# Routing of the first expert half spread over rounds 4 to 8 of the attention, with some of its steps on GpSimd and other places for the gathers

## The chip, the cores and the metric

The kernel runs on one core of one Trainium2 chip. TensorE (PE) multiplies, VectorE (DVE), ScalarE (ACT) and GpSimd (POOL) work element by element, SyncE (SP) only issues DMAs. The metric is the device time of one execution in microseconds (us), as the median of several runs.

## The reference

```python
def _attn_ref(q, k, v, w_phi):                 # q, k, v: 4 x 8 heads x 576 x 64, w_phi: 64 x 128
    def phi(x):
        proj = np.einsum('bhsd,df->bhsf', x, w_phi)
        proj = proj - np.max(np.abs(proj), axis=-1, keepdims=True)
        return np.concatenate([np.exp(proj), np.exp(-proj)], axis=-1)
    q_p, k_p = (phi(q), phi(k))
    kv = np.einsum('bhsf,bhsd->bhfd', k_p, v)
    z = np.sum(k_p, axis=2)
    num = np.einsum('bhsf,bhfd->bhsd', q_p, kv)
    den = np.einsum('bhsf,bhf->bhs', q_p, z)[..., None] + 1e-06
    return (num / den).astype(np.float32)
...
x = np.ascontiguousarray(attn_out.transpose(0, 2, 1, 3)).reshape(B * S, H * D)   # 2304 tokens x 512
logits = x @ w_gate + modality_bias[modality_id]                                 # 8 experts
e_idx = np.argmax(logits, axis=1)
gate_w = probs[np.arange(N), e_idx]
...
    h = np.maximum(x[mask] @ w1[e], 0.0)                                         # per expert, F = 1024
    out[mask] = gate_w[mask, None] * (h @ w2[e])
...
return ((x @ w_a) * (x @ w_b) @ w_out).astype(np.float32)                        # d_ff = 1536
```

## The kernel before

The kernel has three stages, one after the other on TensorE: the attention (to about 167 us), the experts (`Moe`, to about 390 us) and the gated layer (`Moe2`, to the end).

**Attention.** A unit `u` is one pair of batches and one pair of heads; there are eight. `Attn.round(r)` for r = 0 to 8 works on unit r and finishes unit r-1. In a round, `phi` projects a piece of q or k (tile pjp on TensorE; on VectorE the maximum m and the difference df), `turn` transposes parts of df (qtp, then the exponentials qts on ScalarE), `kx` makes the 64x73 products (kxp, copied by VectorE to kx), `vg` the gate products of v (vgp, copied into v), `num` multiplies qts by kx (nmp; VectorE divides: rec, x), and `store` writes x to DRAM (xs) and lets GpSimd add the gate logits (lgp). TensorE's order is that in which the code is written; VectorE, ScalarE, GpSimd and SP are put in an order by a scheduler when the kernel is built. Their order is fixed from then on: each engine runs its list and waits at an instruction until what it needs is there. PSUM tiles come from three pools of two buffers each: pjp, "q" (qtp) and "c" (kxp, vgp, nmp).

**Routing.** The logits of units 0 to 3 are those of the first 1152 tokens, which is half of them. `Route` turns them into tables: `gate` and `score` pick the expert, `rank` counts by matmuls (rkp), `place` and `where` give each token its place (pl, col), `bounds` the tiles' experts and ends (meta), `table` the token of each place (tbp, idx) and `back` the place of each token (tbq, perm, and the gate weights g2). `lookup` is a matmul of one-hot tables. For the first half these are made on GpSimd, by 9 instructions for each table (tbph, tbpl and their product tbpr for `table`; tbqh, tbql, tbqr for `back`). The steps are hung into the rounds by a table: `aside(0)` comes after kx(r-1, 1), `aside(1)` after num and store of unit r-1, `aside(2)` at the end of a round.

**Experts.** A tile is 608 tokens of one expert. `gather` reads its tokens from xs in five indirect DMAs of GpSimd (128 tokens each, the last 96; tile xg), `transp` turns them (mxt on TensorE, then mxh on ScalarE and mxl on VectorE; two PSUM buffers), `l1` and `l2` multiply by weights (hp, yp) that are loaded by SP (s) and split into two parts (wh, wl). The first tile's gathers and transposes lie in the attention's last two rounds. `issue_after(i)` keeps the scheduler from placing an instruction ahead of i; it is no wait on the chip.

Of the kernel before, what the change touches and what calls it, by code (L numbers as in the profile page):

```python
# [12 lines left out]
BF16 = mybir.dt.bfloat16  # L13
I32 = mybir.dt.int32
AF = mybir.ActivationFunctionType
ALU = mybir.AluOpType
# [4 lines left out]
P = 128  # L21
# [4 lines left out]
E = 8  # L26
# [32 lines left out]
class Attn:  # L59
# [159 lines left out]
    def num(self, u, *parts):  # L219
# [20 lines left out]
        for b, h in parts:  # L240
            k = 4 if b < 2 else 2
            nc.vector.tensor_mul(x[:, 4 * b:4 * b + 4, h, :] if b < 2 else x[:, 8, :, :], ps[:, o:o + k, 0:72],
                                 rec[:, o:o + k].unsqueeze(2).to_broadcast([P, k, 72]))
            o += k

    def store(self, u):
# [89 lines left out]
class Route:  # L336
    def __init__(self, tc, pool, lgp, bs, bp):
        self.tc, self.nc = tc, tc.nc
        self.pool, self.lgp, self.bs, self.bp = pool, lgp, bs, bp

    def steps(self, wk, ps, tag, after=None):
# [6 lines left out]
        return [start, self.gate, self.score, self.rank, self.place, self.where, self.bounds, self.table, self.back]  # L348
# [4 lines left out]
    def gate(self):  # L353
        nc, c = self.nc, self.cst
# [6 lines left out]
        nc.vector.tensor_copy(mf, mi)  # L361
        tmp = self.w([NG, E], "bstmp")
        sel = self.w([NG], "bsel")
        for m in range(2):
            nc.vector.tensor_scalar(out=sel, in0=mf, scalar1=float(m), scalar2=None, op0=ALU.is_equal)
            nc.vector.tensor_mul(tmp, sel.unsqueeze(2).to_broadcast([P, NG, E]),
                                 bb[:, m, :].unsqueeze(1).to_broadcast([P, NG, E]))
            nc.vector.tensor_add(lg, lg if m else self.lgp, tmp)
        self.lg = lg

    def score(self):
# [4 lines left out]
        ex = self.w([NG, E], "bstmp")  # L376
# [10 lines left out]
    def rank(self):  # L387
# [9 lines left out]
        gt = self.gt = self.w([NG], "gt")  # L397
        nc.vector.tensor_reduce(out=gt, in_=self.ex, op=ALU.add, axis=AX.X)
        nc.vector.tensor_scalar_add(gt, gt, 1e-9)
        nc.vector.reciprocal(gt, gt)  # L400

    def place(self):
# [8 lines left out]
        pf = self.w([2, E], "pf")  # L411
# [3 lines left out]
        self.tv, self.pf, self.vals = tv, pf, self.w([3, NG], "vals")  # L415
# [33 lines left out]
    def bounds(self):  # L449
        nc, c, tv, pf = self.nc, self.cst, self.tv, self.pf  # L450
# [5 lines left out]
        lo = self.w([NTMAX, E], "lo")  # L456
        hi = self.w([NTMAX, E], "hi")
        te_, of_ = pf[:, 0, :], pf[:, 1, :]
        end = self.w([E], "end")
        nc.vector.tensor_add(end, te_, tv[:, 0, :])  # L460
        it = c["it"].unsqueeze(2).to_broadcast([P, NTMAX, E])
        meta = self.w([3 * NTMAX + 1], "meta")
        nc.vector.tensor_tensor(out=lo, in0=it, in1=te_.unsqueeze(1).to_broadcast([P, NTMAX, E]), op=ALU.is_ge)
        nc.vector.tensor_tensor(out=hi, in0=it, in1=end.unsqueeze(1).to_broadcast([P, NTMAX, E]), op=ALU.is_ge)
        nc.vector.tensor_reduce(out=meta[:, :NTMAX], in_=hi, op=ALU.add, axis=AX.X)
        nc.vector.tensor_scalar(out=meta[:, :NTMAX], in0=meta[:, :NTMAX], scalar1=float(E - 1), scalar2=None, op0=ALU.min)
        nc.vector.tensor_sub(lo, lo, hi)
        b2 = self.w([E], "b2")
        nc.vector.scalar_tensor_tensor(out=b2, in0=te_, scalar=-float(TS), in1=of_, op0=ALU.mult, op1=ALU.add)
        nc.vector.tensor_add(hi, c["ittS"].unsqueeze(2).to_broadcast([P, NTMAX, E]),  # L470
                             b2.unsqueeze(1).to_broadcast([P, NTMAX, E]))
        nc.vector.tensor_mul(hi, hi, lo)
        nc.vector.tensor_reduce(out=meta[:, NTMAX:2 * NTMAX], in_=hi, op=ALU.add, axis=AX.X)
        nc.vector.tensor_scalar(out=meta[:, 2 * NTMAX:3 * NTMAX], in0=meta[:, NTMAX:2 * NTMAX], scalar1=float(CG),
                                scalar2=float(HALF), op0=ALU.add, op1=ALU.min)
        nc.vector.tensor_copy(meta[:, 3 * NTMAX:], end[:, E - 1:E])
# [33 lines left out]
    def table(self):  # L510
# [3 lines left out]
        hi, lo = self.lookup("tbp", self.col, n, self.pl, self.toks)  # L514
        self.token(self.idx, hi, lo, 0)

    def back(self, ps=None, tag=None):
        nc = self.nc
        gp = self.w([3, NG], "gp", BF16)
        rest = self.w([NG], "grest")  # L520
        nc.vector.tensor_copy(rest, self.gt)
        for i in range(3):
            nc.vector.tensor_copy(gp[:, i, :], rest)
            if i < 2:
                nc.vector.tensor_sub(rest, rest, gp[:, i, :])
# [613 lines left out]
```

## Time and profile before

| | us |
|---|---|
| three runs | 814.98, 816.0, 819.0 |
| median | 816.0 |
| the profiled execution | 819.03 |
| its span, first to last instruction | 817.2 |
| mean granted TensorE clock | 0.995 of full speed |

TensorE is busy for 799.0 us of the span, VectorE for 602.8, ScalarE for 376.6 and GpSimd for 136.3. Times in the rows further down are microseconds from the start of the span. In a row of the timeline the bracket tells how long the engine had been idle and which instruction ended that.

### The profile page before, as it was taken

The numbers are of one execution on the slowest core, as the hardware profiler recorded it, in microseconds if no ns is written. First come the engines' busy times: TensorE is split into PE (matmuls) and PEld (weight loads), VectorE is DVE, ScalarE is ACT, GpSimd is POOL, SyncE is SP. The second block draws the span as 40 slices with busy tenths as digits, with TensorE's granted clock in tenths as the row PEclk, the third lists the DMA queues.
The fourth block names the chain that finished last, engine by engine and source line by source line (L and its number), as shares of the span: only waits on it lengthen the run. The fifth ranks groups of instructions, "written<-read, shape, count | busy, mean of one in ns | idle before, by whom it ended". The sixth has DMA issues, their size and how long they took to land.

```text
span 817.2 us, 18324 instructions
## 1 busy us (share of the span) xinstructions
PE 799.0 (98%) x7283; PEld 752.5 (92%) x7284; DVE 602.8 (74%) x1071; ACT 376.6 (46%) x666; POOL 136.3 (17%) x164
## 2 busy tenths in 40 slices
PE   8999998899999999999999999999999999999996
PEld 7999888799999999999999999999999999999995
DVE  6888899599999999974588897764555585544553
ACT  4556544544445555543445444543333364333333
POOL 2000009532326532200112020030000002000002
PEclk9999999999999999999999999999999999999999
DMA  8765432476579887763789787876566658665642
GB/s 304 215 192 162 154 111 82 131 258 198 209 285 338 330 294 274 255 238 114 271 323 364 261 309 260 272 274 202 185 229 205 198 184 302 207 199 193 214 130 89
DMA packets 85163, 184.22 MB, mean 225 GB/s; under 512 B 27760, under 2 KB 37520, under 8 KB 85072
## 3 DMA queue, kind: packets, MB, share of 16 engines
q1 hardware_dynamic: 81872, 173.21, 62.2%
q0 software_dynamic: 3040, 9.72, 3.4%
q8 instruction: 58, 0.95, 0.5%
q14 instruction: 33, 0.27, 0.1%
q10 hardware_dynamic: 160, 0.07, 0.0%
HBM read 145.21 MB, written 37.75 MB: 224 GB/s over the span
## 4 chain that ended last, share of the span: by engine, by line
issue 46%; POOL 3%; PE 2%; POOLq 0%; ACT 0%; ACTq 0%
POOL out L853 2%; POOL cvs L717 1%; PE abp L54 1%; PE abp L56 1%; PE abp L55 1%; POOLq L1136 0%; PE op L55 0%; PE op L54 0%; PE op L56 0%; ACT cvs L716 0%; POOLq L853 0%; POOLq L717 0%; ACTq L884 0%; ACT pc L897 0%
## 5 line engine op out<-in xcount | busy, mean ns | idle before, releaser
L897 ACT COPY pc<-abp 128x384 f32<-128x384 f32 x252 | 120.9, 480 | 193.7 <-PE abp L56 189.7
L54 PE MATMUL abp<-yh,fw 128*128 128x384 f32 x504 | 170.1, 337 | 1.5 <-ACTq L1062 1.0
L56 PE MATMUL abp<-yh,fw 128*128 128x384 f32 x504 | 170.0, 337 | 0.0
L55 PE MATMUL abp<-yl,fw 128*128 128x384 f32 x504 | 169.8, 337 | 0.0
L54 PEld LDWEIGHTS abp<-yh,fw 128*128 128x128 f32 x504 | 94.6, 188 | 10.6 <-ACT pc L897 1.3
L55 PEld LDWEIGHTS abp<-yl,fw 128*128 128x128 f32 x504 | 94.7, 188 | 7.5
L717 POOL TENSOR_SCALAR cvs<-cvs 128x768 f32<-128x768 f32 x24 | 60.3, 2511 | 218.0 <-ACT cvs L716 217.9
L56 PEld LDWEIGHTS abp<-yh,fw 128*128 128x128 f32 x504 | 94.6, 188 | 0.0
L55 PE MATMUL op<-fw,gh 128*128 128x512 f32 x216 | 85.7, 397 | 0.0
L54 PE MATMUL op<-fw,gh 128*128 128x512 f32 x216 | 85.1, 394 | 0.0
L56 PE MATMUL op<-fw,gl 128*128 128x512 f32 x216 | 85.0, 394 | 0.0
L55 PE MATMUL yp<-hl,wh 128*128 128x304 f32 x256 | 77.4, 303 | 0.8 <-DVE hl L608 0.8
L54 PE MATMUL hp<-mxh,wh 128*128 128x304 f32 x256 | 78.0, 305 | 0.0
L55 PE MATMUL hp<-mxl,wh 128*128 128x304 f32 x256 | 77.8, 304 | 0.0
L56 PE MATMUL hp<-mxh,wl 128*128 128x304 f32 x256 | 77.7, 304 | 0.0
L56 PE MATMUL yp<-hh,wl 128*128 128x304 f32 x256 | 77.6, 304 | 0.0
L54 PE MATMUL yp<-hh,wh 128*128 128x304 f32 x256 | 77.0, 303 | 0.0
L853 POOL DMA_INDIRECT out<-o,perm x18 | 18.4, 1020 | 310.6 <-ACT o L852 303.1
L190 ACT ACTIVATE qts<-qtp 128x512 f32<-128x512 f32 (+1 forms) x80 | 38.3, 557 | 58.3 <-PE qtp L187 50.2
L908 DVE TENSOR_TENSOR d<-u,pc 128x768 f32<-128x768 f32 x36 | 34.4, 957 | 28.8 <-ACT pc L897 28.8
L885 DVE TENSOR_TENSOR gl<-ca,gh 128x384 fp32r<-128x384 f32 x72 | 40.8, 574 | 16.4 <-ACT gh L884 15.4
L156 DVE TENSOR_REDUCE m<-pjp 128x8 f32<-128x1024 f32 (+2 forms) x49 | 45.1, 934 | 9.5 <-PE pjp L154 9.5
(191 smaller groups left out, 1595.7 us busy)
## 6 DMA issues: line engine op xcount, KB each, us to landing
fw<-wsc SPq DMA_DIRECT2D x72, 512.0 KB
fw<-wsc SPq DMA_DIRECT2D x144, 256.0 KB
raw<-in_moe_w SPq DMA_DIRECT2D x24, 768.0 KB
s<-in_moe_w SPq DMA_DIRECT2D x32, 512.0 KB
fw<-wsc SPq DMA_DIRECT2D x72, 128.0 KB
wsc<-whi SPq DMA_DIRECT2D x12, 640.0 KB
wsc<-wsum SPq DMA_DIRECT2D x12, 640.0 KB
wsc<-whi SPq DMA_DIRECT2D x12, 512.0 KB
```

What stands on the lines that cost most here:

```text
L54: nc.tensor.matmul(out, lh, rh, start=start, stop=False)
L55: nc.tensor.matmul(out, lh, rl, start=False, stop=False)
L56: return nc.tensor.matmul(out, ll, rh, start=False, stop=stop).ins
L156: nc.vector.tensor_reduce(out=mv, in_=pv, op=ALU.max, axis=AX.X, apply_absolute_value=True)
L190: nc.scalar.activation(t[:, s, :n, :], ps[:, :n, :], AF.Exp, scale=1.0 - 2.0 * s)
L717: nc.gpsimd.tensor_scalar(out=s.bitcast(F32), in0=s.bitcast(F32), scalar1=LEAST, scalar2=None, op0=ALU.max)
L853: st = nc.gpsimd.indirect_dma_start(out=self.out[:, :], out_offset=bass.IndirectOffsetOnAxis(ap=self.routes[bp].perm[:, c:c + 1], axis=0), ...
L885: self.gl = nc.vector.tensor_sub(gl, ca[:, i, :], f32(gh)).ins
L897: self.copied = copied = nc.scalar.copy(x, ps).ins
L908: nc.vector.tensor_add(d, u, x.unsqueeze(1).to_broadcast([P, 2, n]))
```

## The change

The steps of the first half's routing are cut into more pieces and hung elsewhere, some of its arithmetic goes from VectorE to GpSimd, the place of its table tbp in PSUM changes from pool "c" to pool "q", and two things are placed later: the second tile's gathers, and the second transpose of the first tile.

```diff
@@ class Attn
-            nc.vector.tensor_mul(x[...], ps[:, o:o + k, 0:72], ...)
+            self.scaled = nc.vector.tensor_mul(x[...], ps[:, o:o + k, 0:72], ...).ins
...
             if u < 7:
                 self.added = added
+            self.ended = added
@@ class Route
+        self.eng = tc.nc.vector if bp else tc.nc.gpsimd
...
-        return [start, self.gate, self.score, self.rank, self.place, self.where, self.bounds, self.table, self.back]
+        return [start, self.gate, self.score, self.rank, self.place, self.where, self.spans, self.sort, self.bounds, self.table, self.norm, self.back]
@@ gate: modf, bsel, bstmp and lg on eng
-        nc.vector.tensor_copy(mf, mi)
+        eng.tensor_copy(mf, mi)
...
-            nc.vector.tensor_add(lg, lg if m else self.lgp, tmp)
+            eng.tensor_add(lg, lg if m else self.lgp, tmp)
@@ rank: the sum of the exponentials goes to norm
-        gt = self.gt = self.w([NG], "gt")
-        nc.vector.tensor_reduce(out=gt, in_=self.ex, op=ALU.add, axis=AX.X)
-        nc.vector.tensor_scalar_add(gt, gt, 1e-9)
-        nc.vector.reciprocal(gt, gt)
@@ place: only the first of two prefix sums
-        for i in range(2):
-            nc.vector.tensor_mul(big, c["m8"], tv[:, i, :].unsqueeze(1).to_broadcast([P, E, E]))
-            nc.vector.tensor_reduce(out=pf[:, i, :], in_=big, op=ALU.add, axis=AX.X)
+        self.prefix(0)
@@ bounds is cut in three
+    def sort(self):
+        nc, c, pf = self.nc, self.cst, self.pf
         of = self.pick(2, pf[:, 1, :].unsqueeze(1).to_broadcast([P, NG, E]))
         pc = self.w([NG], "pc")
         nc.vector.tensor_add(pc, of, self.vals[:, 0, :])
         self.cq = self.floordiv(pc, c["kp"][:, 1:NG], "cq")
         self.cl = self.over(pc, self.cq, P, "cl")
...
+    def spans(self):
+        nc, c, tv, pf, eng = self.nc, self.cst, self.tv, self.pf, self.eng
+        self.prefix(1)
...
         nc.vector.tensor_add(end, te_, tv[:, 0, :])
         nc.vector.tensor_tensor(out=lo, in0=it, in1=te_.unsqueeze(1).to_broadcast([P, NTMAX, E]), op=ALU.is_ge)
         nc.vector.tensor_tensor(out=hi, in0=it, in1=end.unsqueeze(1).to_broadcast([P, NTMAX, E]), op=ALU.is_ge)
+        eng.tensor_sub(lo, lo, hi)
+        eng.tensor_scalar(out=b2, in0=te_, scalar1=-float(TS), scalar2=None, op0=ALU.mult)
+        eng.tensor_add(b2, b2, of_)
...
+        eng.tensor_mul(span, span, lo)
+        self.hi, self.span, self.end = hi, span, end
+
+    def bounds(self):
+        nc = self.nc
+        meta = self.w([3 * NTMAX + 1], "meta")
+        nc.vector.tensor_reduce(out=meta[:, :NTMAX], in_=self.hi, op=ALU.add, axis=AX.X)
...
@@ Moe.run
-            with behind(at and at.copied, j > 1), behind(at and at.last, j > 2):
+            with behind(at and at.copied, j > 0), behind(at and at.last, j > 2):
                 self.transp(Ts[0], j)
...
                     for i in range(XG):
-                        self.gather(get(n + 1), i)
+                        with behind(at and at.ended, not n):
+                            self.gather(get(n + 1), i)
@@ trn_kernel
-                rsteps = [low(tc, rsteps[0])] + [late(tc, st, at) for st in rsteps[1:7]] + [low(tc, rsteps[7])]
+                rsteps = [(late(tc, st, at, i in (5, 8)) if i not in (0, 9) else low(tc, st)) for i, st in enumerate(rsteps[:11])]
+                rsteps[9] = low(tc, lambda: routes[0].table(at.ps_q, "q"))
...
-            at.round(r, {4: {2: rsteps[:2]}, 5: {0: rsteps[2:3], 2: rsteps[3:5]}, 6: {0: rsteps[5:6], 2: rsteps[6:7]},
-                         7: {0: rsteps[7:8]}, 8: {0: rsteps[8:]}}.get(r, {}) if r > 2 else {})
+            at.round(r, {4: {2: rsteps[:2]}, 5: {0: rsteps[2:3], 2: rsteps[3:5]}, 6: {1: rsteps[5:6], 2: rsteps[6:7]},
+                         7: {0: rsteps[7:8], 1: rsteps[8:10], 2: rsteps[10:11]}, 8: {0: rsteps[11:]}}.get(r, {}) if r > 2 else {})
```

`late(..., scaled)` places a step after the last division x instead of after the last copy kx. `norm` holds the sum of the exponentials and the split of its reciprocal into three bf16 parts (gt, grest, gp). The second half's routing (in the experts' stage) keeps its engine, VectorE, and its places.

What this does to the lists of the engines is told by three places. The first is VectorE in round 6, from the copy kx of unit 5 on. Before:

```order
L214 COPY kx<-kxp 128x292
L438 TENSOR_TENSOR jtc<-vals,kts 128x9
L441 TENSOR_REDUCE jtq<-jtc 128x9
L446 SCALAR_TENSOR_TENSOR rc<-jtq,vals 128x9
L426 TENSOR_TENSOR col<-vals,jtq 128x9
L438 TENSOR_TENSOR jbc<-rc,kp 128x36
L441 TENSOR_REDUCE jbq<-jbc 128x9
L446 SCALAR_TENSOR_TENSOR pl<-jbq,rc 128x9
L427 SCALAR_TENSOR_TENSOR col<-col,jbq 128x9
L156 TENSOR_REDUCE m<-pjp 128x8
```

and with the change, from the last division x of unit 5 on:

```order
L242 TENSOR_TENSOR x<-nmp,rec 128x144
L434 TENSOR_TENSOR jtc<-vals,kts 128x9
...
L434 TENSOR_TENSOR jbc<-rc,kp 128x36
L156 TENSOR_REDUCE m<-pjp 128x8
L437 TENSOR_REDUCE jbq<-jbc 128x9
L157 TENSOR_TENSOR df<-pjp,m 128x1024
L442 SCALAR_TENSOR_TENSOR pl<-jbq,rc 128x9
L423 SCALAR_TENSOR_TENSOR col<-col,jbq 128x9
L214 COPY kx<-kxp 128x292
L447 TENSOR_TENSOR big<-m_1760,tv 128x64
```

The eight instructions of `where` (jtc to col) moved from ahead of the projections phi(1) and phi(3) to behind them and the divisions, and around phi(4). The second place is GpSimd, from the one-hot tables of `table` to the first gathers. Before:

```order
L484 TENSOR_SCALAR tbpl<-i_1744,pl 128x128 x2
L484 TENSOR_SCALAR tbph<-icol,col 128x45 x9
L484 TENSOR_SCALAR tbpl<-i_1744,pl 128x128 x7
L496 TENSOR_TENSOR tbpr<-tbph,tokp 128x9x45 x2
L259 TENSOR_TENSOR lgp_96<-lgp_96,x 128x72
L261 TENSOR_TENSOR lgp_96<-lgp_96,x 128x72
L484 TENSOR_SCALAR tbqh<-icol,cqq 128x9 x9
L484 TENSOR_SCALAR tbql<-i_1744,cl 128x128 x9
L496 TENSOR_TENSOR tbqr<-tbqh,tokp 128x9x9 x2
L496 TENSOR_TENSOR tbqr<-tbqh,gp 128x9x9 x3
L577 DMA xg<-xs_63,idx_2627 128x512 x2
```

and with the change:

```order
L492 TENSOR_SCALAR tbpl<-i_1744,pl 128x128 x7
L470 TENSOR_TENSOR b_2508<-b_2508,pf 128x8
L468 TENSOR_TENSOR lo<-lo,hi 128x72
L504 TENSOR_TENSOR tbpr<-tbph,tokp 128x9x45 x2
L471 TENSOR_TENSOR span<-ittS,b_2508 128x72
L473 TENSOR_TENSOR span<-span,lo 128x72
L492 TENSOR_SCALAR tbqh<-icol,cqq 128x9 x9
L492 TENSOR_SCALAR tbql<-i_1744,cl 128x128 x9
L504 TENSOR_TENSOR tbqr<-tbqh,tokp 128x9x9 x2
L259 TENSOR_TENSOR lgp_96<-lgp_96,x 128x72
L592 DMA xg<-xs_63,idx_2721 128x512 x2
```

The gathers stand behind the one-hots of both tables in either list; four small instructions of `spans` came between, and the three products with gp moved behind the gathers. The third place is TensorE from the last product kxp of round 7 on. Before:

```order
L589 MATMUL mxt<-ident,xg 128x128 x8
L231 MATMUL nmp<-kx,qts 64x73 x32
L187 MATMUL qtp<-ident,df 128x128 x8
L589 MATMUL mxt<-ident,xg 128x128 x4
```

and with the change:

```order
L604 MATMUL mxt<-ident,xg 128x128 x4
L231 MATMUL nmp<-kx,qts 64x73 x32
L187 MATMUL qtp<-ident,df 128x128 x8
L604 MATMUL mxt<-ident,xg 128x128 x6
```

Four transposes are one gather's. The first gather's still stand ahead of the product nmp of unit 7, the second's moved behind it.

## Rows read from the trace of the kernel before

**Rows 1.** The page: busy time, share of the span and instructions by engine

```profile
PE 799.0 (98%) x7283; PEld 752.5 (92%) x7284; DVE 602.8 (74%) x1071; ACT 376.6 (46%) x666; POOL 136.3 (17%) x164
```

**Rows 2.** Windows by round: stretch, us, busy by engine (instructions), clock, DMA, GB/s

```profile
71.60:89.75 18.15, 18.15 (x434) 16.97 (x430) 15.08 (x29) 10.15 (x18) 0.81 (x3) 1.00 0.55 171
89.75:110.41 20.66, 18.59 (x436) 17.27 (x434) 17.37 (x43) 10.52 (x19) 0.47 (x2) 1.00 0.48 150
110.41:130.43 20.02, 18.71 (x446) 17.45 (x444) 18.87 (x58) 10.27 (x18) 8.49 (x18) 1.00 0.32 91
130.43:151.50 21.07, 19.75 (x446) 18.09 (x442) 18.97 (x50) 10.26 (x18) 15.75 (x34) 1.00 0.38 107
```

**Rows 3.** Timeline of TensorE: start, us, instruction and count [idle before, ended by]

```profile
113.93 0.21 PE L391 MATMUL rkp<-oh,ltri 128*128 128x80 bf16 x1 [0.27 <-DVE x L242]
...
126.82 1.09 PE L187 MATMUL qtp<-ident,df 128*128 128x128 f32 x8 [1.04 <-DVE df L157]
...
133.98 1.24 PE L231 MATMUL nmp<-kx,qts 128*64 128x73 f32 x32 [1.31 <-DVE meta L466]
...
151.50 1.62 PE L589 MATMUL mxt<-ident,xg 128*128 128x128 f32 x8
155.00 3.59 PE L231 MATMUL nmp<-kx,qts 128*64 128x73 f32 x64 [1.88 <-DVE kx L214]
...
167.10 0.38 PE L54 MATMUL hp<-mxh,wh 128*128 128x304 f32 x1
```

**Rows 4.** Timeline of VectorE, rounds 6 to 8

```profile
120.61 0.16 DVE L438 TENSOR_TENSOR jtc<-vals,kts 128x9 f32<-128x9 f32 x1
...
128.26 1.21 DVE L156 TENSOR_REDUCE m<-pjp 128x8 f32<-128x1024 f32 x1
...
131.03 1.30 DVE L431 TENSOR_TENSOR sel<-oh,pf 128x72 f32<-128x72 bf16 x1
...
133.54 0.29 DVE L199 COPY v<-vgp 128x144 f32<-128x144 f32 x1
...
154.39 0.46 DVE L214 COPY kx<-kxp 128x292 f32<-128x292 f32 x1 [3.03 <-PE mxt L589]
...
164.64 0.68 DVE L593 TENSOR_TENSOR mxl<-mxt,mxh 128x512 fp32r<-128x512 f32 x1
```

**Rows 5.** Timeline of GpSimd: one-hot tables, their products, the first gathers

```profile
121.94 1.21 POOL L484 TENSOR_SCALAR tbpl<-i,pl 128x128 bf16<-128x128 f32 x2 [13.21 <-DVE col L427]
...
130.51 1.68 POOL L496 TENSOR_TENSOR tbpr<-tbph,tokp 128x405 bf16<-128x405 bf16 x2
132.15 0.37 POOL L259 TENSOR_TENSOR lgp<-lgp,x 128x72 f32<-128x72 f32 x1
...
134.29 2.69 POOL L484 TENSOR_SCALAR tbqh<-icol,cqq 128x9 bf16<-128x9 f32 x9 [1.32 <-DVE cqq L441]
136.94 5.25 POOL L484 TENSOR_SCALAR tbql<-i,cl 128x128 bf16<-128x128 f32 x9
142.13 0.62 POOL L496 TENSOR_TENSOR tbqr<-tbqh,tokp 128x81 bf16<-128x81 bf16 x2
...
143.73 1.11 POOL L577 DMA_INDIRECT xg<-xs,idx  x1
```

**Rows 6.** The gathers' DMA queue by 147.0 and by 149.5 us: packets, MB, share

```profile
q0 software_dynamic: 88, 0.29, 27.3%
q0 software_dynamic: 160, 0.52, 27.8%
```

**Rows 7.** Windows in the last round (columns as rows 2)

```profile
154.40:157.70 3.30, 2.70 (x45) 2.73 (x46) 1.81 (x4) 1.07 (x2) 1.90 (x2) 0.50 0.45 138
157.70:167.10 9.40, 9.11 (x213) 8.45 (x211) 5.62 (x20) 4.43 (x7) 2.30 (x13) 0.99 0.46 119
```

**Rows 8.** SP's issue of the first weights, and what their queue moved from 140 to 142 us

```profile
137.67 0.90 SPq L560 DMA_DIRECT2D s<-in_moe_w  x2
...
q1 hardware_dynamic: 270, 0.76, 100.6%
```

More of the change, by code (lines that the diff above doesn't have):

```diff
@@ L447, in over, with prefix @@
         return t
-    def bounds(self):
-        nc, c, tv, pf = self.nc, self.cst, self.tv, self.pf
+    def prefix(self, i):
+        nc, big = self.nc, self.w([E, E], "big")
+        nc.vector.tensor_mul(big, self.cst["m8"], self.tv[:, i, :].unsqueeze(1).to_broadcast([P, E, E]))
+        nc.vector.tensor_reduce(out=self.pf[:, i, :], in_=big, op=ALU.add, axis=AX.X)
+    def sort(self):
+        nc, c, pf = self.nc, self.cst, self.pf
         of = self.pick(2, pf[:, 1, :].unsqueeze(1).to_broadcast([P, NG, E]))
@@ L455, in bounds @@
         self.cl = self.over(pc, self.cq, P, "cl")
[L456 to L457 removed]
+    def spans(self):
+        nc, c, tv, pf, eng = self.nc, self.cst, self.tv, self.pf, self.eng
+        self.prefix(1)
         te_, of_ = pf[:, 0, :], pf[:, 1, :]
[L459 removed]
+        lo, hi, span = (self.w([NTMAX, E], n) for n in ("lo", "hi", "span"))
+        end, b2 = self.w([E], "end"), self.w([E], "b2")
+        it = c["it"].unsqueeze(2).to_broadcast([P, NTMAX, E])
@@ new lines, in spans @@
+        eng.tensor_scalar(out=b2, in0=te_, scalar1=-float(TS), scalar2=None, op0=ALU.mult)
+        eng.tensor_add(b2, b2, of_)
+        eng.tensor_add(span, c["ittS"].unsqueeze(2).to_broadcast([P, NTMAX, E]),
+                       b2.unsqueeze(1).to_broadcast([P, NTMAX, E]))
+        eng.tensor_mul(span, span, lo)
[4 more added lines that the diff above has]
+        nc.vector.tensor_reduce(out=meta[:, :NTMAX], in_=self.hi, op=ALU.add, axis=AX.X)
+        nc.vector.tensor_scalar(out=meta[:, :NTMAX], in0=meta[:, :NTMAX], scalar1=float(E - 1), scalar2=None, op0=ALU.min)
+        nc.vector.tensor_reduce(out=meta[:, NTMAX:2 * NTMAX], in_=self.span, op=ALU.add, axis=AX.X)
@@ L513, in table, with norm @@
         self.idx = self.pool.tile([P, n], I32, name=f"idx{self.bp}")
-        hi, lo = self.lookup("tbp", self.col, n, self.pl, self.toks)
+        hi, lo = self.lookup("tbp", self.col, n, self.pl, self.toks, ps, tag)
         self.token(self.idx, hi, lo, 0)
-    def back(self, ps=None, tag=None):
+    def norm(self):
         nc = self.nc
-        gp = self.w([3, NG], "gp", BF16)
+        gt = self.gt = self.w([NG], "gt")
+        nc.vector.tensor_reduce(out=gt, in_=self.ex, op=ALU.add, axis=AX.X)
+        nc.vector.tensor_scalar_add(gt, gt, 1e-9)
+        nc.vector.reciprocal(gt, gt)
+        gp = self.gp = self.w([3, NG], "gp", BF16)
         rest = self.w([NG], "grest")
@@ L942, in low, with late @@
     return run
-def late(tc, step, at):
+def late(tc, step, at, scaled=False):
     def run():
-        with tc.high_priority(offset=-LOWR), tc.issue_after(at.copied):
+        with tc.high_priority(offset=-LOWR), tc.issue_after(at.scaled if scaled else at.copied):
             step()
```

34 lines of the change are left out of this document (13 added, 21 removed).

## Prediction

> **What bounds the kernel now.** I read the busy shares first, then windows by round, then the timelines of TensorE, VectorE and GpSimd where a round is longer than its neighbour. TensorE is busy for 98% of the span [rows 1], so time can only come from places where it waits, or works at the lower clock. Rounds 5, 6 and 7 last 20.66, 20.02 and 21.07 us where the round ahead of them lasts 18.15 [rows 2]: 2.51 + 1.87 + 2.92 = 7.3 us too much together. In these rounds VectorE is busy for 17.37 to 18.97 us against 15.08 in round 4: the routing's small steps stand between its attention work, and TensorE waits for what is queued behind them. The TensorE timeline names three such waits [rows 3]: 0.27 us for x at 113.93, 1.04 us for df at 126.82, and 1.31 us at 133.98, the last put down to meta. They are 2.62 us in all, the most that a better place of the steps can give there.
>
> The fourth hole is at the end. After the last product kxp of round 7 TensorE turns the first two gathers (mxt, 151.50) and then stands idle for 1.88 us until the copy kx; nmp resumes at 155.00 [rows 3]. Then the granted clock is 0.50 for 3.30 us, which is the 1.2 GHz level, and 0.99 afterwards [rows 7]. In that stretch nmp's 64 matmuls take 3.59 us, where 32 take 1.24 at 133.98 [rows 3]: about 1.3 is the clock's. The experts' first product hp starts at 167.10, which is 12.1 us after the resume. Whatever the change does ends in that number: behind hp the lists of the engines are nearly the same. So I walk along the changed lists with the durations of before, and ask when hp starts.
>
> **The change, round by round.** *gate on GpSimd* (7 small operations) ends ahead of round 5's matmuls of the routing; no wait of TensorE above belongs to it: 0. *The sum of the exponentials* (gt and its split) leaves the stretch ahead of the 0.27-us wait [rows 3], so that wait goes. I count 0.24 of it, since VectorE waits for rkp next.
>
> *where* is eight instructions, from jtc at 120.61 to pl and col; GpSimd's first one-hot follows at 121.94 [rows 4, 5]. That is 1.22 us of VectorE gone from ahead of the projections, and the df that TensorE waits for at 126.82 comes more than 1.04 us earlier: gain 1.04. The price is that the eight now start behind the divisions and around phi(4). The m of phi(4) is at 128.26 [rows 4]; moved up by 1.38 (1.22 + part of 0.27) it would be at 126.88, where jtc now starts in its place. With m and df (1.21 each) between the last of the eight, pl and col are ready at 126.88 + 1.22 + 2 x 1.1 = 130.3, against 121.9 before: **8.4 us later**. (I take 1.1 as the step from start to start, since starts lie closer than durations.)
>
> *bounds* stood ahead of the copy v at 133.54, which ends the gate's PSUM tile; its part ahead of v begins at 131.03 (sel), 2.51 us [rows 4]. Five small instructions of spans stand there now, about 0.2 each, 0.95. The 1.31-us wait goes. Taken with the 1.04 and the 0.24, TensorE runs about 2.0 us ahead through round 7; not the full 2.6, since pl now delays the copy kx by about 0.5.
>
> *tbp in pool "q".* The matmuls of tbp take the slot that two transposes later qtp needs, and it is free only when idx is copied. In the changed list of VectorE idx stands behind the divisions of unit 6, at about 147.2 by the walk, while TensorE would be at that qtp at 145.9. A new wait of about 1.4 us, so TensorE comes to the end of round 7's kxp at about 150.6, where before it was there at 151.50 [rows 3]: 0.9 is left of 2.0.
>
> *GpSimd's chain.* It starts with pl and col at 130.3 and has to go through both tables before the first gather, as before. The steps: one-hots of the token table 121.94 to 130.51, 8.57; four operations of spans in the shape of lgp, 0.37 each, with their gaps 4 x 0.42 = 1.7; the products tbpr 1.64 (1.68); tbqh 134.29 to 136.94, 2.65; tbql 136.94 to 142.13, 5.19; tbqr 0.55; lgp 0.4 [rows 5]. Sum 20.7, so the first gather begins at 130.3 + 20.7 = **151.0**, where before it was 143.73. The sort on VectorE gives cqq near 140, ahead of tbqh at 142.2, so it costs nothing; were it 3 us later, it would all go to the gather. The only slack of the old chain was 1.32 us of waiting for cqq and one lgp.
>
> *Landing.* A gather's 80 packets: 88 were done by 147.0 and all 160 of two gathers by 149.5 [rows 6]. The first began at 143.73 and so took at most 3.3, the second, which began some 1.2 later (its issue takes 1.11 [rows 5]), at most 4.6. Bounds 3.1 to 4.3; the data are there between 154.1 and 155.3. The Trainium skill ("DMA: Bandwidth & Descriptors", the fit for a gpsimd DMA) gives 2.0 us + bytes / 436e3, an estimate of 2.6 us for 0.26 MB; by it the sum would be 0.9 lower, and this trace shows a longer one. Four transposes and their start add 0.7 (8 take 1.62 [rows 3]), so nmp resumes between 154.8 and 156.0; I take **155.2**, against 155.00. TensorE's list has mxt ahead of nmp: it has to stand still from 150.6, 3.9 us and more, and I expect the low clock once more.
>
> *From the resume to hp.* 12.1 us before. The second gather's transposes, four, are now behind nmp: they were half of a batch of 1.62 us ahead of it [rows 3], of which 0.7 stays ahead; part of them fills waits behind nmp, +0.3. The last transposes share two PSUM buffers; mxt of the fourth gather needs the buffer that mxl of the second (0.68 us, at 164.64 before [rows 4]) gives back. On VectorE's list that mxl has moved behind the two wl, each a 128x1024 operation like m (1.21 [rows 4]), and three small ones: late by some 1.2 + 0.6, of which 1.0 is slack: +0.8, bounds 0 and 1.8. So hp starts at 155.2 + 13.2 = 168.4 against 167.10, **+1.3 us**.
>
> *The later gathers.* Five gathers of tile 1 at some 1.2 us each stand in front of GpSimd's work of the next stage. Nothing is read from them until the second tile: 0, at most 1. *meta* comes at 147.7, so SP issues the first weights at about 150.5 instead of 137.67 [rows 8]. hp needs them at 168: hidden, but they now share queues with the gathers (a rival below).
>
> The profiled execution lasted 819.03, so the changed one would last 820.3. The median of three is 816.0, which gives 817.3 with the same difference. The runs at 815 may lack the hole at 155 with its slow clock; then 816.0 is a kernel that resumes some 2 to 3 us earlier, and the changed one, which is held by the gather in any case, stays at 820. I take the middle: **819.0**. The own range of this case is 816.5 to 822.5.
>
> **A rule to weigh.** The selection sel takes 1.30 us at 131.03 beside GpSimd's product tbpr, where the small operations of these rows take 0.16 to 0.46 [rows 4, 5]. The Trainium skill ("SBUF — State Buffer", who interferes with whom) says that VectorE and GpSimd lock a shared port: a VectorE operation with two SBUF inputs and a GpSimd operation that reads SBUF exclude each other for the whole instruction. The trace agrees here, with 1.30 us. It speaks against moving more to GpSimd; by it the first gather could be up to 8 x 0.2 us = 1.6 later (an estimate). By the rows alone, where only one operation shows it, 0 to 1 us, and I leave it in the range.
>
> **The rivals.**
> - *Faster: the gather lands in time.* If GpSimd's chain goes 3.9 us faster than my sum (first gather at or before 147.1), the data land before TensorE gets to mxt; then it doesn't stop, and the low clock's 1.3 us go too. hp would come at 150.6 + 0.7 + 13.2 - 1.3 = 163.2, 3.9 earlier: 812.1 from the median, 815.1 from the profiled execution, middle 813.6. For it: the chain is one-hots of equal size with hardly any data dependence. Against it: these are the very durations of [rows 5], and pl has an m and a df in the middle. 0.10.
> - *Slower: gathers and weights meet.* The weight loads are issued at 150.5, the first gather at 151.0. At 140 to 142 the same loads moved 0.76 MB at 100.6% of the queues [rows 8]. If the gather's packets stand behind them, it lands 1.0 to 2.7 us later; at 2.7 the low clock stands longer as well (+1.6). 821.3 to 824, middle 822.3. It decides from a resume at 156.0 on. Against it: the gather has a queue of its own, q0 at 27% [rows 6]. 0.25.
> - *Slower: the hole before kx stays.* The copy kx began at 154.39 after 3.03 us of idle, put down to mxt [rows 4], and a hole of 2.8 us there has no cause that I can name. If it belongs to the transposes of gathered data and returns behind them, 819.0 + 2.8 = 822 to 823. 0.10.
> - The forecast 0.55.
>
> **How the numbers follow.** 0.5% of 816.0 is 4.1 us, about what a measurement of this kernel can tell from no change: faster means under 811.9, slower over 820.1. The faster rival puts half of its 0.10 below 811.9: 0.05, and 0.01 of the forecast. The slower side has the 0.35 of two rivals, nearly all, and a little of the forecast's upper end: 0.37. No change gets 0.57. The range is 813.5 to 824.0: it takes in the middle of the fast rival and the upper end of the meeting of DMAs, and leaves out about 0.1 at either end together.
>
> **What the profile would show.** Right: no wait of TensorE over 0.5 us for df or meta in rounds 6 and 7, these rounds shorter by about 1.2 and 0.8; pl at about 130 and the first gather at about 151; a qtp that waits 1.4 us for idx near 147; nmp resuming near 155 after mxt, then a clock of 0.5; hp near 168.4. Wrong: a first gather before 148, nmp resuming before 152, or a clock that stays near 1.0 in that stretch. In these cases the kernel is faster. A gather that takes over 5 us to land beside the loads s is the second rival.

## The result, and the profile after

The changed kernel takes 824.12 us (median; 823.97 to 824.87) against 816.45 of the kernel before in the same comparison: ratio 1.0095, 95% interval 1.0076 to 1.0114. It is slower by 7.7 us. The forecast was 819.0 with a range up to 824.0.

The profiled execution of the changed kernel lasted 823.97 us (span 822.2), 4.9 more than the profiled one of before (819.03), which was the longest of its runs. So I begin with a second profile of the kernel before, an execution of 816.02 us (span 814.2). The profiles of this document reach the same early place at 105.54 to 109.12 us, so I measure from one place that all kernels share, the transposes qtp of round 5 (106.80 in the first profile).

| run (us) | qtp, round 5 | nmp resumes, from there | hp starts, from there | hp to first abp |
|---|---|---|---|---|
| before, as in the rows ahead | 106.80 | 48.20 | 60.30 | 225.97 |
| before, second profile | 108.21 | 45.39 | 55.81 | 225.94 |
| changed | 108.24 | 50.36 | 61.74 | 227.97 |

abp is the first matmul of the third stage (393.07 in the first profile); the spans behind it differ by under 0.2 us. TensorE's first and last rows of that reading, in the second profile of before and in the changed kernel:

```profile
108.21 1.09 PE L187 MATMUL qtp<-ident,df 128*128 128x128 f32 x8 [0.48 <-DVE df L157]
389.96 0.44 PE L54 MATMUL abp<-yh,fw 128*128 128x384 f32 x1 [1.02 <-ACTq L1062]
```

```profile
108.24 1.09 PE L187 MATMUL qtp<-ident,df 128*128 128x128 f32 x8 [0.48 <-DVE df L157]
397.95 0.44 PE L54 MATMUL abp<-yh,fw 128*128 128x384 f32 x1 [1.03 <-ACTq L1079]
```

Against the second profile the change costs 4.97 up to the resume, 0.96 from there to hp, and 2.03 behind hp: 7.96 together, close to the 7.7 between the medians.

Windows of the changed kernel, with the limits of [rows 2] moved by 1.44 us (rounds 5 to 7):

```profile
91.19:111.85 20.66, 18.39 (x432) 17.07 (x429) 16.11 (x36) 10.52 (x19) 2.45 (x9) 1.00 0.49 150
111.85:131.87 20.02, 19.85 (x482) 18.49 (x478) 17.69 (x48) 10.28 (x18) 1.11 (x4) 1.00 0.32 94
131.87:152.94 21.07, 17.62 (x353) 16.02 (x355) 19.23 (x47) 10.26 (x18) 20.79 (x46) 0.93 0.13 31
```

In the second row TensorE has 482 matmuls in the stretch that held 446 before, and VectorE 1.2 us less work: round 6 did what the change says. In the third row more than that is lost: 353 matmuls instead of 446, at a mean clock of 0.93, and GpSimd is busy for 20.79 of 21.07 us. The timeline of TensorE in the changed kernel tells where:

```profile
132.26 2.25 PE L231 MATMUL nmp<-kx,qts 128*64 128x73 f32 x64 [0.51 <-DVE big L447]
...
145.73 1.16 PE L154 MATMUL pjp<-wp,qk 64*128 64x128 f32 x16 [0.45 <-DVE df L157]
148.12 0.63 PE L187 MATMUL qtp<-ident,df 128*128 128x128 f32 x4 [1.23 <-DVE rec L238]
150.14 1.09 PE L187 MATMUL qtp<-ident,df 128*128 128x128 f32 x4 [1.39 <-DVE meta L480]
...
158.01 0.66 PE L604 MATMUL mxt<-ident,xg 128*128 128x128 f32 x4 [3.10 <-DMA xg<-xs,idx]
158.60 2.25 PE L231 MATMUL nmp<-kx,qts 128*64 128x73 f32 x64
...
169.98 0.39 PE L54 MATMUL hp<-mxh,wh 128*128 128x304 f32 x1
...
173.02 0.55 PE L54 MATMUL hp<-mxh,wh 128*128 128x304 f32 x2 [1.12 <-ACT mxh L607]
186.09 0.38 PE L54 MATMUL hp<-mxh,wh 128*128 128x304 f32 x1 [1.09 <-DVE hl L623]
```

The waits of [rows 3] at 113.93, 126.82 and 133.98 are gone but for 0.51. In their place TensorE waits 1.23 and 1.39 us at qtp, and then at mxt for the first gather. GpSimd in the changed kernel, from the one-hots to that gather and to the clamps cvs:

```profile
131.77 1.22 POOL L492 TENSOR_SCALAR tbpl<-i,pl 128x128 bf16<-128x128 f32 x2 [1.96 <-DVE col L423]
...
152.19 1.12 POOL L592 DMA_INDIRECT xg<-xs,idx  x1 [0.17 <-issue]
...
179.48 4.29 POOL L733 TENSOR_SCALAR cvs<-cvs 128x768 f32<-128x768 f32 x2
```

The chain begins at 131.77 where it began at 121.94, and the first gather at 152.19 where it began at 143.73 [rows 5]. From its start to the transposes 5.82 us go by. SP now issues the two weight loads at 152.54, beside it, and in the two microseconds from 154 the queues of the changed kernel moved this (packets, MB, share):

```profile
152.54 0.90 SPq L575 DMA_DIRECT2D s<-in_moe_w  x2
...
q1 hardware_dynamic: 133, 0.48, 64.4%
q0 software_dynamic: 46, 0.19, 29.8%
```

The queue of the gathers, q0, got 29.8% of the time and the weights' queue 64.4%.

VectorE in the changed kernel has two operations of 128x9 elements that last as long as the GpSimd work beside them, and two that take longer than the 0.18 us of such a cast at 156.26:

```profile
140.71 1.82 DVE L454 TENSOR_TENSOR pc<-vals 128x9 f32<-128x9 f32 x1
...
179.56 2.15 DVE L533 COPY grest<-gt 128x9 f32<-128x9 f32 x1
181.74 0.77 DVE L535 CAST gp<-grest 128x9 bf16<-128x9 f32 x1
...
182.75 1.05 DVE L535 CAST gp<-grest 128x9 bf16<-128x9 f32 x1
```

The first ends with the two products tbpr, the second with the first of the two clamps, which are done at 183.77 together. The two casts stand beside the second clamp; there VectorE was held only in part.

### The profile page after: what moved, and what is told of

Read it like the earlier page. It is cut to its first block, busy times and chain, and to the rows that moved or that the text cites. A ratio compares the mean times of both kernels' runs of the same rounds, so it can differ in the third digit from the quotient of the medians.

```text
span 822.2 us, 18330 instructions
## 1 busy us (share of the span) xinstructions
PE 799.3 (97%) x7284; PEld 752.1 (91%) x7284; DVE 603.7 (73%) x1061; ACT 376.3 (46%) x666; POOL 139.0 (17%) x176
## 4 chain that ended last, share of the span: by engine, by line
PE 34%; issue 16%; ACT 1%; DVE 1%; POOL 1%; POOLq 0%; DVEq 0%
PE abp L54 7%; PE abp L56 7%; PE abp L55 7%; PE op L55 4%; PE op L54 4%; PE op L56 4%; POOL out L869 1%; ACT pc L913 0%; DVE gl L901 0%; DVE ca L899 0%; ACT yh L813 0%; DVE o L866 0%; POOLq L1153 0%; ACT gh L900 0%; DVE ca L929 0%
## 5 line engine op out<-in xcount | busy, mean ns | idle before, releaser
L733 POOL TENSOR_SCALAR cvs<-cvs 128x768 f32<-128x768 f32 x24 | 58.6, 2443 | 215.3 <-ACT cvs L732 215.2
```

The costliest lines, as they stand in the source:

```text
L733: nc.gpsimd.tensor_scalar(out=s.bitcast(F32), in0=s.bitcast(F32), scalar1=LEAST, scalar2=None, op0=ALU.max)
```

## The experiments

Each ratio is to the kernel before on the same chip in the same comparison. There were four comparisons. The kernel before took 816.14 us in the one with its own second profile, the weights out of the gather's way, where back behind kx, and the changed kernel without the late gathers; 820.06 in the one with where and table back, only the second tile's gathers late, only the second transposes late, and the kept parts; 815.35 in the one with the first two gathers late, the clamp in halves, and three gathers ahead; and 815.57 in that of the last run. So absolute times of different comparisons are not set side by side. Stretches of the profile are taken from qtp of round 5, as above. Where an edit names steps of the list, step 5 is where, 6 spans, 7 sort, 8 bounds, 9 table, 10 norm.

**The kernel before again.**

> The kernel before, once more, for a second profile. The profiled execution of before lasted 819.03 us, the other runs 814.98 to 816.9. Theory A: the 2.8-us hole ahead of the copy kx near 154 and the clock of 0.50 behind it belong to the slow execution only; a run near 816 then shows nmp resuming near 152 at full clock. Theory B: both are in every run, and the 3 us between the runs lie elsewhere (the stretch behind 390 us, or the start).

816.02 us. TensorE in it:

```profile
152.58 1.09 PE L589 MATMUL mxt<-ident,xg 128*128 128x128 f32 x8
153.60 2.25 PE L231 MATMUL nmp<-kx,qts 128*64 128x73 f32 x64
...
164.02 0.38 PE L54 MATMUL hp<-mxh,wh 128*128 128x304 f32 x1
```

Theory A, as far as one more profile shows it. There is no stop behind mxt, and nmp's 64 matmuls take 2.25 us instead of 3.59: the hole of 1.88 us and the stretch at a clock of 0.50 in [rows 3, 7] are not in every execution. This one reaches hp 4.49 us earlier than the rows that I summed from.

**Only the first two gathers late.** The edit moves the second along with the first; the others stood there before.

```diff
 (before)   for j in range(XG):
-                with behind(at and at.added, j > 1):
+                with behind(at and at.added, True):
                     self.gather(get(0), j)
```

> The kernel before with one thing moved: the first two gathers stand behind the logits lgp of unit 6 on GpSimd and so begin near 150 instead of 143.7; the weight loads s stay early (137.7). Theory A (a first gather that begins at 150 stops TensorE, and without weight loads beside it it lands in some 3.3 us): mxt waits for DMA until about 153.5, nmp resumes near 155 to 156, 2 to 3 us more than the kernel before. Theory B (a gather takes 5.8 us to land there whatever else moves): mxt near 156, nmp near 157 to 158, 4 to 6 us more. Theory C (the wait is hidden): no change.

821.45 us, ratio 1.0084 (1.0060 to 1.0108). GpSimd and TensorE in it:

```profile
151.91 1.11 POOL L577 DMA_INDIRECT xg<-xs,idx  x1 [0.61 <-DMA xs<-x]
```

```profile
155.53 0.66 PE L589 MATMUL mxt<-ident,xg 128*128 128x128 f32 x4 [2.80 <-DMA xg<-xs,idx]
156.98 0.66 PE L589 MATMUL mxt<-ident,xg 128*128 128x128 f32 x4 [0.80 <-DMA xg<-xs,idx]
157.57 2.25 PE L231 MATMUL nmp<-kx,qts 128*64 128x73 f32 x64
```

Theory A for the landing, and the loss is larger than it said, as large as theory B had put it: late first gathers, all else untouched, give most of the ratio of the whole change (1.0095). In this profile hp comes 3.91 us later than in the second profile of before (59.72 against 55.81); the median loses 6.1, which this one execution does not show. Without weight loads beside it the gather takes 3.62 us to the transposes.

**Weights out of the gather's way.**

```diff
 (changed)
-           7: {0: rsteps[7:8], 1: rsteps[8:10], 2: rsteps[10:11]}
+           7: {0: rsteps[7:9], 1: rsteps[9:10], 2: rsteps[10:11]}
```

bounds is placed after the last copy kx here, not after the last division x.

> The changed kernel with bounds (meta) already behind kx in round 7, so that SP issues the first two weight loads s some 6 us earlier, ahead of the first gathers instead of beside them. Theory A (gathers and weight loads meet in the DMA queues): the first gather's data are there about 3.3 us after it begins instead of 5.8, mxt starts near 155.5 instead of 158.0, the time falls by about 2.5 us to 821.6. Theory B (a gather takes 5.8 us there for its own reasons): mxt near 158, 824. The transposes of the second gather stand ahead of nmp again in this kernel, which moves 0.7 us from behind nmp to ahead of it.

822.95 us, ratio 1.0076 (1.0059 to 1.0093). SP issues s at 142.88, and GpSimd and TensorE show:

```profile
151.28 1.12 POOL L592 DMA_INDIRECT xg<-xs,idx  x1 [0.17 <-DVE df L157]
```

```profile
154.94 0.98 PE L604 MATMUL mxt<-ident,xg 128*128 128x128 f32 x4 [2.70 <-DMA xg<-xs,idx]
157.18 1.11 PE L604 MATMUL mxt<-ident,xg 128*128 128x128 f32 x4 [1.25 <-DMA xg<-xs,idx]
158.22 4.02 PE L231 MATMUL nmp<-kx,qts 128*64 128x73 f32 x64
```

In the two microseconds from 153, which begin 1.7 us behind the gather's start (1.8 in the two shown for the changed kernel), the queue of the gathers moved more than twice as many packets:

```profile
q0 software_dynamic: 110, 0.39, 73.1%
```

For the landing theory A holds: 3.66 us instead of 5.82. For the time it does not: TensorE waits for the second gather, whose transposes stand ahead of nmp here, and nmp then takes 4.02 us, at the lower clock (granted 0.50 from 158.2 to 160).

**where back behind kx.**

```diff
 (changed)
-           6: {1: rsteps[5:6], 2: rsteps[6:7]}
+           6: {0: rsteps[5:6], 2: rsteps[6:7]}
```

where is placed after the last copy kx again, not after the last division x.

> The changed kernel with the step where (pl, col) back behind kx in round 6, all else as changed. Theory A (the late pl starts GpSimd's chain late and the chain sets the first gather): one-hots start near 122 instead of 131.8 and end near 143; the first gather is then no longer held by GpSimd but by idx, which VectorE's list has at 149.8, so it starts at about 150 instead of 152.2, the wait of about 1 us for df near 126.8 comes back, and the time falls by about 2 us, to 822. Theory B (where's place does not count, the landing of the gathers beside the weights does): one-hots early, yet the transposes mxt start within 0.5 us of 158.0 and the time stays at 824.

823.47 us, ratio 1.0082 (1.0065 to 1.0099). GpSimd and TensorE in it:

```profile
141.27 2.70 POOL L492 TENSOR_SCALAR tbqh<-icol,cqq 128x9 bf16<-128x9 f32 x9 [7.67 <-DVE cqq L437]
...
150.20 1.12 POOL L592 DMA_INDIRECT xg<-xs,idx  x1 [0.17 <-issue]
```

```profile
156.22 1.11 PE L604 MATMUL mxt<-ident,xg 128*128 128x128 f32 x4 [4.73 <-DMA xg<-xs,idx]
157.27 3.90 PE L231 MATMUL nmp<-kx,qts 128*64 128x73 f32 x64
```

The one-hots begin at 121.45 and the first gather at 150.20, the times of theory A. But it is not idx that holds the gather (idx is ready at 148.03), and from qtp of round 5 (106.80 here) it begins at 43.40, where it begins at 43.95 in the changed kernel: 0.55 us earlier and not 2. The one-hots tbqh, which stand ahead of it in GpSimd's list, wait 7.67 us for cqq: the sort, which the change hangs into round 7, holds them almost as long as the late pl did. The weight loads moved with the gather (issued at 150.58) and it took 6.02 us to land, and nmp lost 1.65 us to the clock (3.90 us, granted 0.50 from 157.27 to 159). The 2 us did not come.

**where and table back, table in pool c.** where is placed after the last copy kx here too.

```diff
 (changed)
-           6: {1: rsteps[5:6], 2: rsteps[6:7]}, 7: {0: rsteps[7:8], 1: rsteps[8:10], 2: rsteps[10:11]}
+           6: {0: rsteps[5:6], 2: rsteps[6:7]}, 7: {0: rsteps[7:8] + rsteps[9:10], 1: rsteps[8:9], 2: rsteps[10:11]}
-           rsteps[9] = low(tc, lambda: routes[0].table(at.ps_q, "q"))
+           rsteps[9] = low(tc, routes[0].table)
```

> The changed kernel with where behind kx in round 6 and with the token table back behind kx in round 7 and in pool c, all else as changed (sort, spans, norm, gate, late meta, the late second transpose, the late gathers of the second tile). Theory A (the loss up to hp is the late first gather): idx near 141, first gather near 142, no stop of TensorE ahead of mxt, nmp resumes some 5 us earlier than in the changed kernel; what stays is the stretch behind hp (1.1 for mxh, 1.1 for hl): 817. Theory B (the stop has another cause, weights or the clock): mxt still waits, over 820.

820.75 us, ratio 1.0008 (0.9993 to 1.0024). First gather at 142.25, mxt at 151.60 without a wait: theory A. Nearly the whole loss is gone with the early tables, though the weight loads are as late as in the changed kernel (152.21). From hp to abp it still takes 227.40. TensorE waits for mxh there, and not for hl:

```profile
170.38 0.55 PE L54 MATMUL hp<-mxh,wh 128*128 128x304 f32 x2 [1.50 <-ACT mxh L607]
```

The second tile's gathers are late in this kernel too, and a copy grest of 2.66 us stands beside the first clamp. But the second clamp begins 0.57 us after the first has ended, and no wait of TensorE follows.

**Only the second tile's gathers late.**

```diff
 (before)           for i in range(XG):
-                       self.gather(get(n + 1), i)
+                       with behind(at and at.ended, not n):
+                           self.gather(get(n + 1), i)
```

> The kernel before with one part of the change: the second tile's gathers behind the last lgp. Theory A (GpSimd's clamps cvs are pushed together behind five gathers and block VectorE beside them): cvs starts near 177 instead of 172 to 174, one or two VectorE copies of 2 us beside it, a wait of about 1 us for hl near 184, 817.1. Theory B (hidden, as predicted): 816.1.

822.94 us, ratio 1.0029 (1.0015 to 1.0043). VectorE, GpSimd and TensorE in it:

```profile
178.22 2.66 DVE L522 COPY grest<-gt 128x9 f32<-128x9 f32 x1
180.91 2.07 DVE L524 CAST gp<-grest 128x9 bf16<-128x9 f32 x1
```

```profile
178.67 4.28 POOL L719 TENSOR_SCALAR cvs<-cvs 128x768 f32<-128x768 f32 x2
```

```profile
185.68 0.38 PE L54 MATMUL hp<-mxh,wh 128*128 128x304 f32 x1 [2.62 <-DVE hl L609]
```

Theory A, and more than it said (it had one wait of about 1 us). The first copy ends with the first clamp, the second with the second; wl and hl stand behind them. From hp to abp 228.58 us, 2.6 more than before.

**The same with the clamp in two halves.**

```diff
-       nc.gpsimd.tensor_scalar(out=s.bitcast(F32), in0=s.bitcast(F32), scalar1=LEAST, scalar2=None, op0=ALU.max)
+       for c in (s[:, :384], s[:, 384:]):
+           nc.gpsimd.tensor_scalar(out=c.bitcast(F32), in0=c.bitcast(F32), scalar1=LEAST, scalar2=None, op0=ALU.max)
```

> The kernel before with the second tile's gathers late, as in the run of that part alone, and with GpSimd's clamp cvs of 128x768 cut into two of 128x384 (1.07 us each). Theory A (a VectorE copy between SBUF tiles is blocked for the whole of the GpSimd instruction beside it): no VectorE copy longer than about 1.3 us beside the clamps where there were copies of 2.66 and 2.07, but as many GpSimd us as before, so the wait for hl goes from 2.6 to between 1.5 and 2.6. Theory B (the copies are slow for another reason, such as the gathers' DMA traffic): copies of 2 us and more again.

815.54 us, ratio 0.9996 (0.9982 to 1.0009): the loss is gone. GpSimd's first clamps and the longest of VectorE's small copies beside them:

```profile
174.46 5.43 POOL L720 TENSOR_SCALAR cvs<-cvs 128x384 f32<-128x384 f32 x4
```

```profile
175.06 0.65 DVE L524 CAST gp<-grest 128x9 bf16<-128x9 f32 x1
```

It went further than theory A: no wait for hl behind hp at all. Four halves took 5.43 us, where two whole ones took 4.28, so by these times GpSimd waited too, and the two engines took turns. From hp to abp 225.71. The run with whole clamps belongs to another comparison; each is set against its own kernel before.

**The changed kernel without the late gathers of the second tile.**

```diff
 (changed)
-                       with behind(at and at.ended, not n):
-                           self.gather(get(n + 1), i)
+                       self.gather(get(n + 1), i)
```

> The changed kernel without the condition that the second tile's five gathers stand behind the last lgp. Theory A (GpSimd's clamp cvs starts 5.5 us late, at 179.5, and blocks VectorE's small copies beside it): cvs back near 174 to 177, no grest of 2.15 us and no wait for hl near 186, time 1.1 us shorter, 823.0. Theory B (VectorE's list is late anyway and the gathers cost nothing): the same wait of 1.1 us at 186, 824.

822.87 us, ratio 1.0072 (1.0055 to 1.0089). Behind hp theory A holds: the wait at 186 is gone and hp to abp is 225.99, as before the change. Up to hp this execution took 2.3 us more than the changed kernel's, most of it from the clock (nmp 3.95 us, granted 0.50 from 159.1 to 161), so the profiled times are alike. By time alone the two kernels are not told apart: their intervals overlap.

**Only the second transposes late.**

```diff
 (before)
-           with behind(at and at.copied, j > 1), behind(at and at.last, j > 2):
+           with behind(at and at.copied, j > 0), behind(at and at.last, j > 2):
```

> The kernel before with one part of the change: the second gather's transposes behind the copy kx. Theory A (as predicted for the changed kernel: part of the transposes and one wait for mxl, +0.3 and +0.5, and since the products of the second half of the tokens come earlier in TensorE's list, a wait for mxh of about 1.1 behind hp): 817.5 to 818. Theory B (it costs nothing, since four transposes more fit behind nmp): 816.1.

820.2 us, ratio 1.0008 (0.9990 to 1.0027). The interval takes in both theories; the stretch behind hp speaks for theory B. TensorE does wait 1.14 us for mxh behind hp, as theory A had it, but hp to abp is 226.06: the wait for hl at yp that the kernel before has some 35 us later (0.84 and 0.64 us in its two profiles) is not there. One wait took the place of another.

**The parts that looked worth keeping.** gate, norm, spans and sort as changed; where, bounds and table early, the table in pool c; the second transposes and the second tile's gathers as before; where and bounds after the last copy kx.

```diff
 (changed)
-           6: {1: rsteps[5:6], 2: rsteps[6:7]}, 7: {0: rsteps[7:8], 1: rsteps[8:10], 2: rsteps[10:11]}
+           6: {0: rsteps[5:6], 2: rsteps[6:7]}, 7: {0: rsteps[7:10], 2: rsteps[10:11]}
```

> As the kernel before with only these parts of the change: gate on GpSimd, norm and spans and sort spread over later rounds. where, table, bounds, the second transpose and the second tile's gathers stand as early as they can. Theory A: the waits of 0.27 at 113.9 and of 1.31 at 134 go, nothing comes in their place, the time is 816.1 - 1.3 = 814.8, or 814 with the clock at full. Theory B (every us that a round gains is lost again later, since the first transposes or kx wait): 816.

819.24 us, ratio 0.9993 (0.9978 to 1.0008), which takes in both theories (A meant 0.998). No stop ahead of nmp, but the third gather, behind lgp, now comes too late for a TensorE that is 0.7 us earlier at the first mxt (43.64 from qtp of round 5, against 44.37):

```profile
155.09 0.63 PE L604 MATMUL mxt<-ident,xg 128*128 128x128 f32 x4 [1.61 <-DMA xg<-xs,idx]
```

**Three gathers ahead of the one-hots of back.** As the last, and:

```diff
-           with behind(at and at.added, j > 1):
+           with behind(at and at.added, j > 2):
                self.gather(get(0), j)
```

> The kept parts (gate on GpSimd, norm, spans, sort spread; tables early) and the third gather right behind the first two, ahead of the one-hots of back. In the run of the kept parts the third gather began at 151.6 behind lgp and TensorE, now earlier, waited 1.6 us for it at 155.1. Theory A: that wait goes, nothing takes its place, 1.5 us less than the run of the kept parts in the same comparison with the kernel before: ratio 0.997. Theory B (the next wait, on weights or on kx, takes it): ratio 0.999.

815.63 us, ratio 0.9999 (0.9987 to 1.0012): theory B. The next wait is for the products with gp, which stand behind the gathers:

```profile
159.62 0.39 PE L508 MATMUL tbq<-tbqr,tbql 128*128 128x45 bf16 x9 [2.41 <-POOL tbqr L504]
```

**norm earlier.** As the last, and norm after the last division x:

```diff
-           7: {0: rsteps[7:10], 2: rsteps[10:11]}
+           7: {0: rsteps[7:10], 1: rsteps[10:11]}
```

> As the run with three gathers ahead of the one-hots, and norm directly behind the divisions of unit 6 instead of behind kx of round 7, so that the three products of the gate weights (tbqr with gp) stand ahead of the last gathers on GpSimd. In the run before this one TensorE waited 2.41 us at 159.6 for these products. Theory A: the wait goes and hp comes some 2 us earlier; ratio to the kernel before about 0.997, faster. Theory B (the next thing, weights or the tokens' transposes, takes the place): ratio 0.9995 to 1.

818.79 us, ratio 1.0039 (1.0026 to 1.0053): slower, which neither theory had. VectorE and TensorE in it:

```profile
153.04 1.41 DVE L535 CAST gp<-grest 128x9 bf16<-128x9 f32 x1
...
155.14 0.45 DVE L214 COPY kx<-kxp 128x292 f32<-128x292 f32 x1
```

```profile
155.74 4.12 PE L231 MATMUL nmp<-kx,qts 128*64 128x73 f32 x64 [3.44 <-DVE kx L214]
```

The small copies of norm now stand ahead of kx and beside GpSimd's one-hots; a cast of 128x9 takes 1.41 us, kx comes late, TensorE waits 3.44 us and then runs at the lower clock (granted 0.50 from 157 to 159). None of the versions beats the kernel before beyond its interval.

## Why the prediction was wrong, step by step

**The rounds.** Right for round 6: the waits for x, df and meta are gone, and it is shorter. Wrong for round 7, which I had shorter too. Up to the last kxp I had TensorE 0.9 us ahead; it was about 2 us behind (kxp ends at 154.91, which is 153.47 on the clock of [rows 3]). I had 1.4 us for "idx in pool q", and the wait at 150.14 is 1.39, right behind idx (149.80, 0.19 us). The 1.23 at 148.12 and 0.45 at 145.73 were not in my sum, nor was the clock, which is 0.50 and 0.68 in the two windows from 150 to 154. The sum has a slip as well: 2.0 less 1.4 is 0.6, and I went on with 0.9. All this cost nothing, since TensorE had 3.10 us to wait for the gather behind it.

**GpSimd's chain.** Right. First gather predicted at 151.0, measured 150.75 (152.19 less 1.44). The sort, which I had ready near 140, came with nothing to spare: cqq at 143.13, tbqh at 143.23. With an early pl it holds the chain by itself. That late first gathers are what counts is shown from both sides: alone they cost 0.8%, and with the early tables nearly the whole loss goes.

**Landing.** The first step that failed, by size: 3.1 to 4.3 us was forecast for the landing; 5.82 went by up to the transposes, and nmp resumed at 157.16 on that clock where I had 155.2, 2.0 later. This is the rival "gathers and weights meet" (+1.0 to 2.7), to which I gave 0.25. With the weights issued earlier the same gather took 3.66, in the kernel before with late gathers 3.62. I had counted the late meta as hidden because hp needs the weights only at 168; that was true of the weights, and not of the gather that they now meet. The Trainium skill ("DMA: Bandwidth & Descriptors", the fit for a gpsimd DMA) makes 2.6 us of 0.26 MB, an estimate. The runs show more, up to the start of the transposes: 3.62 and 3.66 us without weight loads beside the gather, 5.82 to 6.02 with them. What the landing alone costs in time is not shown, since the run with earlier weights lost its gain again at the second gather.

**From the resume to hp.** Right as a difference: 11.38 against 10.42, +0.96, where +1.1 was forecast. Wrong as a sum: I had put the 1.1 on 12.1, a stretch with the low clock in it, and expected that clock again. It did not fall there (nmp 2.25 us). In this execution it had fallen ahead of the stop, from 150 on. In the run without the late gathers of the second tile, whose TensorE list up to hp is the same, it was at 1.00 from 150 to 154 and fell in the stop, and hp came 64.05 us behind qtp of round 5 instead of 61.74.

**The later gathers.** The second step that failed: "0, at most 1". Alone they cost 0.3% (2.4 to 2.9 us). In the changed kernel the stretch behind hp is 2.03 us longer, and without the late gathers it is not. I asked only who reads the gathers' data, and not what stands behind them on GpSimd: two clamps, pushed together, that block VectorE's copies. Not all of the 2.03 is shown to be theirs: of the two waits of TensorE behind hp, 1.09 us is for hl, and the other, 1.12 us for mxh, lies ahead of the clamps. The rule I weighed, the Trainium skill's on the shared port ("SBUF — State Buffer", who interferes with whom: one holds it for its whole instruction, the other fully blocks), was at work at a place where I had not looked. I had told it of operations with two inputs, and these copies have one; the same section says that copies and casts can contend too. The trace agrees in the main: copies of 2.15, 2.66 and 2.07 us beside clamps of 2.14 (that of 2.66 began 0.45 ahead of its clamp, while the last gather was still being issued), and none over 0.65 beside halves. In all five runs that have the late gathers and whole clamps a copy of 2.15 to 2.66 us stands beside the first clamp; in the eight with early gathers no operation of 128x9 beside a clamp takes over 0.82. The casts of 0.77 and 1.05 us beside the changed kernel's second clamp do not fit a block for the whole instruction.

**The base.** The third step that failed, and the largest. I had hp at 168.4, which is 61.6 from qtp of round 5; it came at 61.74. That is luck: the two errors on the way, 2.0 more for the landing and the low clock that stayed away in this execution, nearly cancel. But I set it against the 60.30 of one profiled execution with a hole of 1.88 us and a stretch at half clock. I saw that the 815 us runs "may lack" both, wrote that the changed kernel then "stays at 820", and took the middle. The second profile lacks them: from its 55.81 my own hp is 5.8 us late, not 1.3, and with the 2.0 behind hp that is 7.8, where 7.7 were measured. The run with the clamp in halves, whose TensorE list up to hp is that of the kernel before, has 55.81 as well. How usual the hole is was not measured. In the comparison in which the kernel before took 820.06 the two runs that leave its routing alone (the second tile's gathers late, the second transposes late) both have it, so there it may be no exception.

**The chances.** Slower had 0.37; it was nearly all the sum of two rivals with 0.25 and 0.10, and the first of these happened on top of the forecast, not in its place. By its own terms its upper end was 820.3 + 2.7 + 1.6 = 824.6, and I wrote 824. The fast rival did not happen: TensorE waited.

Open: what ends the hole ahead of kx that some executions have and others of the same list do not (the kernel before: 1.88 us and none; two of the experiments 1.83 and 2.37). The row names mxt, which had ended at 153.12 in the rows ahead, 1.27 us before the copy. VectorE is not alone in it: in all three profiles with that hole ScalarE starts 0.06 us behind the copy kx, after 4.06 to 4.09 us of idle. Open too is how the 6.1 us that the median loses to a late first gather divide, since its profiled execution was one of the shorter ones (819.89 of 819.4 to 825.84).

## What to carry to other kernels

When a step is moved back, follow each thing that it feeds to the queue it ends in, and ask what it will now stand beside: weights beside a gather, clamps beside copies. A transfer that nobody waits for can still be the neighbour of one that TensorE waits for. And before a sum is made on one profiled execution, compare its time with the others: a profile 3 us above the median may hold waits that other executions lack.

## What the runs showed of the hardware that was not expected

A GpSimd tensor_scalar of 128x768 held a VectorE copy of 36 bytes per partition for its whole 2.14 us where the copy came at its start, and not always so (casts of 0.77 and 1.05 us beside one); cut in two it cost 0.65 at most, and the kernel got back 0.3%. In six of the profiles TensorE's clock is at 0.50 behind a stop of 1.9 to 4.7 us ahead of nmp, so that nmp's 64 matmuls take 3.6 to 4.1 us instead of 2.25. In three others, with stops of 1.83, 2.80 + 0.80 and 3.10 us at the same place (the second transposes late, the first two gathers late, the changed kernel), it is at 1.00. Such a stop costs its own length, and in most of these profiles 1.3 to 1.9 us more behind it.
